# One ordered list for the attention and the start of the MLP, with the layer norm and the first weights in it

## The chip, the core and the metric

The kernel runs on one core of a Trainium2 chip. The metric is the device time of one launch in microseconds (us), lower is better. Times of single instructions are in nanoseconds (ns). The engines are named as in the profile: PE (TensorE, matmuls and transposes), DVE (VectorE), ACT (ScalarE), POOL (GpSimd) and SP (SyncE, which issues the loads and stores).

## The reference

Three stages in a row, with 4 batches, 8 heads, 576 tokens and a model width of 512:

```python
# 1. local attention: 4 heads see the last 32 tokens, 4 heads every 4th of the last 128
scores = np.where(masks[None], scale * np.matmul(q, k.transpose(0, 1, 3, 2)), -1e9)
attn = np.exp(scores - scores.max(-1, keepdims=True))
attn = attn / (np.sum(attn, axis=-1, keepdims=True) + 1e-09)
x = np.matmul(attn, v)                       # then heads side by side: (4, 576, 512)
# 2. mixture of 4 causal attention experts, 2 of 4 chosen for each token by a gate
a = softmax(causal(scale * (x @ wq[e]) @ (x @ wk[e]).T))
out += mask[..., None] * w[:, :, kk:kk + 1] * (a @ (x @ wv[e]) @ wo[e])
# 3. layer norm and MLP with a residual
xn = (x - mu) / np.sqrt(var + 1e-06) * g_ln
return x + np.maximum(xn @ w_ch1, 0.0) @ w_ch2
```

The two MLP weights arrive as 64-bit floats.

## The kernel before

Stage 1 runs in windows of three blocks of 64 queries by 96 keys for two heads (`window`, 48 of them). A window subtracts the row maximum on DVE, takes the exponential on ACT, sums on DVE (L439), adds 1e-9 to the sums on DVE (L441), takes the reciprocal (L443), multiplies on DVE or POOL (L445), transposes on PE and multiplies by the values. Stage 2 projects the result to values and gate (`value_tile`, tile `pv`), and to queries and keys (`project`, tile `pp`, L609); `attend` makes scores `s`, the softmax (L694 to L728), the transposes `ph` and `ppt` and the product `py`; `out_proj` (L823, tile `pwo`) gives the tokens `x2a` and `x2b` and their mean and variance. Values that need more than one pass are kept as a high and a low part, so most products are three matmuls.

Stage 3 works on 18 tiles of 128 tokens in five groups, `gi` 0 to 3 of four tiles and `gi` 4 of two. `norm` takes the mean off (tile `xg`, a single buffer, L971), transposes on PE (`pxt`, L974) and splits the result in high and low part (`xn`, ACT L982 and DVE L983). The hidden width is cut in 16 pieces `f`; each piece has two weight blocks which `decode` turns from 64-bit words into high and low parts: one step on ACT (L910), then DVE, POOL, DVE, ACT and POOL in turn (L911 to L922). `mlp_group` makes the hidden values (`phid`, L998), a ReLU in two parts (`ht`, L1005 and L1006), the output (`pout`, L1016) and adds it to the tokens on DVE (L1018). `inverse_std` has one POOL power (L946).

What sets the order: stages 1 and 2 are generators that ask for one operation at a time, with an engine (or a choice of two), a cost in ns and the times of what they depend on. `run_chains` always takes the operation that could begin first by these costs, at equal times the one with the lower rank, and the order in which it takes them is the order of each engine's instructions (`manual_schedule`). Stage 3 of the kernel before is recorded behind that list, as streams whose shares are set by the table `PRM`, and the layer below the kernel puts these instructions where its own scheduler wants them; they begin among the attention steps of the last batch. After its first three groups for `f` 0 to 2, the rest of stage 3 is a list of jobs in a fixed order, the same in both kernels: pieces 0 and 1 for groups 3 and 4, then piece 3, then pieces 2 and 3, then pairs of pieces for all five groups.

Of the kernel before, what the change touches and what calls it, by code (L numbers as in the profile page):

```python
# [23 lines left out]
def windowed_attention_moe_mlp(  # L24
# [20 lines left out]
    P = 128  # L45
# [110 lines left out]
    places = {"a": [0.0] * BANKS["a"], "s": [0.0] * BANKS["s"], "t": [0.0] * BANKS["t"]}  # L156
    facts, chains, mode = {}, [], [None]
# [38 lines left out]
    def run_chains():  # L196
        while chains:
# [50 lines left out]
    def attention_weights(x):  # L248
# [36 lines left out]
    places.update(nat=[0.0] * 2, vt=[0.0] * 2, qT=[0.0] * 2, sc=[0.0] * 5, pT=[0.0] * 2, xh=[0.0] * XB)  # L285
# [110 lines left out]

    def window(b, hp, u):
# [35 lines left out]
        sc = win.tile([P, TU, 96], F32, tag="sc", name="sc", bufs=5)  # L433
# [10 lines left out]
        t, e = yield either(("DVE", 370.0), ("POOL", 620.0), deps=[t])  # L444
# [8 lines left out]
        give("sc", t)  # L453
        pT = win.tile([96, TU * P], F32, tag="pT", name="pT", bufs=2)
# [37 lines left out]
    def value_tile(b, i):  # L492
# [19 lines left out]
        yield op("DVE", 75.0, [t, tv])  # L512
        nc.vector.tensor_copy(Gb[:m, i], pv[:m, E * D:NV])
# [3 lines left out]
        else:  # L517
# [63 lines left out]
    def project(b, pr_):  # L581
# [18 lines left out]
        for hf in range(2):  # L600
            for wh, wl, isq in ((wkh, wkl, False), (wqh, wql, True)):
# [10 lines left out]
                done_x(b, t)  # L612
                ends = []
# [37 lines left out]
    def attend(b, pr_, i):  # L651
# [64 lines left out]
        t = yield op("DVE", 75.0, tsum)  # L716
# [86 lines left out]
    def out_proj(b, i):  # L803
# [55 lines left out]
    phase_w.close()


    streams, done = {}, set()

    def add(key, gen, start, end, work):
        streams[key] = [gen, start, (end - start) / work]

    def step(key):
        st = streams[key]
        try:
            st[1] += next(st[0]) * st[2]  # L870
        except StopIteration:
            del streams[key]
            done.add(key)

    def need(key):
        while key not in done:
            step(key)

    def run_until(end):
        while streams:  # L880
            key = min(streams, key=lambda x: streams[x][1])
            if streams[key][1] >= end:
                break
            step(key)

    def after(keys, make):
        for key in keys:
            need(key)
        yield from make()


    wts = ctx.enter_context(tc.tile_pool(name="wts", bufs=1, side="right", reuse_waits="tile"))
    GF = 2
    groups = [range(a, min(a + 4, NTT)) for a in range(0, NTT, 4)]
    EARLY = 3
    g_in = wts.tile([P, KC], F32, name="g_in")
    nc.sync.dma_start(g_in, g_ln.rearrange("(c p) -> p c", p=P))
    w1v = w_ch1.bitcast(I32)
    w2v = w_ch2.bitcast(I32)

    def decode(src, hi, lo, gain):

        nl, nh = src[:, :, 0], src[:, :, 1]
        sq = wts.tile([P, DM], F32, tag="d_sq", name="d_sq", bufs=1)
        t1 = wts.tile([P, DM], I32, tag="d_t1", name="d_t1", bufs=1)
        pw = wts.tile([P, DM], I32, tag="d_pw", name="d_pw", bufs=1)
        nc.scalar.activation(sq, nh.bitcast(F32), AF.Square)  # L910
        nc.vector.tensor_scalar(t1, nh, 3, 0x3FFFFFF8, op0=ALU.logical_shift_left, op1=ALU.bitwise_and)  # L911
        nc.vector.scalar_tensor_tensor(t1, nh, -0x40000000, t1, op0=ALU.bitwise_and, op1=ALU.bitwise_or)  # L912
        nc.vector.tensor_scalar(pw, t1, -0x800000, None, op0=ALU.bitwise_and)
        pf = pw.bitcast(F32)
# [194 lines left out]
```

## Time and profile before

| | |
|---|---|
| median of 3 runs | 785.63 us (783.86 to 786.97) |
| the profiled execution | 782.97 us |
| its span, first to last instruction | 780.9 us |
| PE busy | 731.1 us (94%) |
| DVE busy | 555.5 us (71%) |
| ACT busy | 296.5 us (38%) |
| POOL busy | 212.4 us (27%) |
| mean granted TensorE clock | 0.980 |

The profiled execution took 2.07 us beyond its span. Busy time is the time in which at least one instruction of the engine ran; a busy PE can still run below its best rate. The granted clock is a share of 2.4 GHz.

### The profile page before, as it was taken

The numbers are of one execution on the slowest core, as the hardware profiler recorded it, in microseconds if no ns is written. First come the engines' busy times: TensorE is split into PE (matmuls) and PEld (weight loads), VectorE is DVE, ScalarE is ACT, GpSimd is POOL, SyncE is SP. The second block draws the span as 40 slices with busy tenths as digits, with TensorE's granted clock in tenths as the row PEclk, the third lists the DMA queues.
The fourth block names the chain that finished last, engine by engine and source line by source line (L and its number), as shares of the span: only waits on it lengthen the run. The fifth ranks groups of instructions, "written<-read, shape, count | busy, mean of one in ns | idle before, by whom it ended". The sixth has DMA issues, their size and how long they took to land.

```text
span 780.9 us, 13839 instructions
## 1 busy us (share of the span) xinstructions
PE 731.1 (94%) x5196; PEld 607.2 (78%) x5196; DVE 555.5 (71%) x1420; ACT 296.5 (38%) x796; POOL 212.4 (27%) x247
## 2 busy tenths in 40 slices
PE   6698989998998878799999999999999999999997
PEld 5577768987897667677778788888888888888886
DVE  5776988699968899889667897866466475553333
ACT  3455756556655654545224222222121121211110
POOL 3151422113412344333202344424033141220000
PEclk9979989999999989999999999999999999999999
DMA  7671323213120201101000121211011020000114
GB/s 150 130 145 39 74 64 68 52 41 82 42 54 13 65 28 55 55 1 55 1 1 28 54 81 56 81 54 60 22 54 55 4 78 27 28 1 0 40 69 134
DMA packets 87889, 41.79 MB, mean 54 GB/s; under 512 B 74384, under 2 KB 83088, under 8 KB 87824
## 3 DMA queue, kind: packets, MB, share of 16 engines
q1 hardware_dynamic: 87824, 40.92, 19.9%
q8 instruction: 41, 0.67, 0.4%
q14 instruction: 24, 0.20, 0.1%
HBM read 36.19 MB, written 4.72 MB: 52 GB/s over the span
## 4 chain that ended last, share of the span: by engine, by line
PE 70%; DVE 20%; ACT 4%; issue 2%; DMA 1%; POOL 1%; SPq 1%; DVEq 0%; POOLq 0%; ACTq 0%
PE phid L998 25%; PE pout L1016 25%; PE pp L609 4%; PE pwo L823 3%; PE ppt L750 2%; DVE sc L434 2%; DVE mx L431 2%; DVE sm L439 2%; DVE xl L484 1%; PE pv L508 1%; PE py L772 1%; DVE nm L694 1%; PE ppt L452 1%; DVE SQ L621 1%; PE ptr L372 1%
## 5 line engine op out<-in xcount | busy, mean ns | idle before, releaser
L1016 PE MATMUL pout<-wp,ht 128*128 128x512 f32 x864 | 215.8, 395 | 0.3 <-DVE ht L1006 0.3
L998 PE MATMUL phid<-xn,wp 128*128 128x512 f32 (+1 forms) x960 | 214.8, 372 | 0.0
L998 PEld LDWEIGHTS phid<-xn,wp 128*128 128x128 f32 x960 | 168.9, 188 | 34.8 <-DVE xn L983 0.2
L1016 PEld LDWEIGHTS pout<-wp,ht 128*128 128x128 f32 x864 | 160.2, 188 | 36.6 <-DVE ht L1006 0.8
L1018 DVE SCALAR_TENSOR_TENSOR x2a<-pout,rstd,x2a 128x512 f32<-128x512 f32 x124 | 88.4, 745 | 77.6 <-PE pout L1016 77.3
L1005 ACT ACTIVATE ht<-phid 128x512 fp32r<-128x512 f32 (+1 forms) x80 | 44.4, 555 | 222.3 <-PE pout L1016 137.0
L922 POOL TENSOR_TENSOR wp<-d_pw,wp 128x512 fp32r<-128x512 f32 x34 | 46.9, 1380 | 139.8 <-ACT wp L921 128.8
L728 POOL TENSOR_SCALAR Pp<-Pp,rs 128x128 f32<-128x128 f32 (+3 forms) x44 | 49.9, 1138 | 112.5 <-DVE rs L721 67.3
L1006 DVE SCALAR_TENSOR_TENSOR ht<-phid,ht 128x512 fp32r<-128x512 f32 (+1 forms) x80 | 50.1, 632 | 39.0 <-ACT ht L1005 38.8
L916 POOL TENSOR_TENSOR d_pw<-d_pw,d_t 128x512 f32<-128x512 f32 x34 | 44.0, 1294 | 70.1 <-DVE d_pw L915 57.8
L445 POOL TENSOR_TENSOR sc<-sc,rs 128x288 f32<-128x288 f32 x38 | 25.2, 670 | 85.0 <-DVE rs L443 36.7
L234 ACT COPY pT<-ppt 96x384 f32<-96x384 f32 (+4 forms) x79 | 35.9, 461 | 14.6 <-PE ppt L750 10.5
L696 ACT ACTIVATE Pp<-s,nm 128x192 f32<-128x192 f32 (+3 forms) x64 | 30.3, 474 | 23.4 <-DVE nm L694 19.7
L921 ACT CAST wp<-d_pw 128x512 fp32r<-128x512 f32 x34 | 21.1, 620 | 42.0 <-DVE d_pw L917 35.3
L679 PE MATMUL s<-KH,SQ 128*128 128x64 f32 (+4 forms) x96 | 34.0, 362 | 2.7 <-ACT Pp L696 2.3
L910 ACT ACTIVATE d_sq<-ws 128x512 f32<-128x512 f32 x34 | 22.9, 674 | 35.0 <-DVE d_pw L917 29.8
L452 PE MATMUL ppt<-ident,sc 128*96 128x128 f32 x144 | 25.5, 294 | 10.8 <-POOL sc L445 7.0
L372 PE MATMUL ptr<-ident,nat 72*128 72x72 f32 (+1 forms) x196 | 25.4, 253 | 10.5 <-DMA nat<-in_q_dram 8.3
L912 DVE SCALAR_TENSOR_TENSOR d_t<-ws,d_t 128x512 int32<-128x512 int32 x34 | 34.5, 1016 | 0.6
L423 PE MATMUL s<-kT,qT 64*64 64x96 f32 x576 | 34.1, 258 | 0.3 <-ACT kT L234 0.2
L750 PE MATMUL ppt<-ident,Pp 128*128 128x128 f32 x160 | 30.3, 290 | 3.0 <-DVE klz L630 1.3
L423 PEld LDWEIGHTS s<-kT,qT 64*64 64x64 f32 x576 | 31.3, 145 | 0.9 <-issue 0.5
(164 smaller groups left out, 1377.5 us busy)
## 6 DMA issues: line engine op xcount, KB each, us to landing
ws<-in_moe_w_ch_dram SPq DMA_DIRECT2D x34, 512.0 KB, 3.4
nat<-in_q_dram SPq DMA_DIRECT2D x14, 288.0 KB, 3.5
nat<-in_k_dram SPq DMA_DIRECT2D x14, 288.0 KB
vt<-in_v_dram SPq DMA_DIRECT2D x16, 192.0 KB, 4.2
out_dram<-x2a SPq DMA_DIRECT2D x12, 256.0 KB, 2.1
vt<-in_v_dram SPq DMA_DIRECT2D x32, 48.0 KB, 2.0
out_dram<-x2b SPq DMA_DIRECT2D x4, 256.0 KB, 2.5
vt<-in_v_dram SPq DMA_DIRECT2D x16, 40.0 KB, 1.9
```

Source lines behind the costliest of these rows:

```text
L234: (nc.scalar.copy if engine == "ACT" else nc.vector.tensor_copy)(dst, src)
L423: nc.tensor.matmul(ps[z, 96 * tt:96 * (tt + 1)], qT[z, 64 * t_:64 * t_ + 64], kT[z, 64 * t_:64 * t_ + 96], start=False, stop=tt == TU - 1)
L728: (nc.vector if e == "DVE" else nc.gpsimd).tensor_scalar(Ps[ee][:m, 64:n], Ps[ee][:m, 64:n], rs[:m, ee:ee + 1], None, op0=ALU.mult)
L750: nc.tensor.transpose(pt[:, P * (j - 1):P * j], Ps[ee][:, k0:k0 + P], ident)
L912: nc.vector.scalar_tensor_tensor(t1, nh, -0x40000000, t1, op0=ALU.bitwise_and, op1=ALU.bitwise_or)
L916: nc.gpsimd.tensor_tensor(pf, pf, t1.bitcast(F32), op=ALU.add)
L922: nc.gpsimd.tensor_tensor(lo, pf, hi.bitcast(F32), op=ALU.subtract)
L998: nc.tensor.matmul(ph[:, :n_tok], ws[:, c * P:(c + 1) * P], xs[c], start=n == 0, stop=n == 3 * KC - 1)
L1005: nc.scalar.activation(hh[:, :n_tok], ph[:, :n_tok], AF.Relu)
L1006: nc.vector.scalar_tensor_tensor(hl[:, :n_tok], ph[:, :n_tok], 0.0, hh[:, :n_tok].bitcast(F32), op0=ALU.max, op1=ALU.subtract)
L1016: nc.tensor.matmul(po, a_[:, sl], w_, start=n == 0, stop=n == 3 * len(fs) - 1)
L1018: nc.vector.scalar_tensor_tensor(x2(i), po, rstd[:, i:i + 1], x2(i), op0=ALU.mult, op1=ALU.add)
```

## The change

- **One list.** Opening the weights' memory, the decoding of the first three pieces (`decode`), `inverse_std`, `norm` for all five groups, and the first three groups for pieces 0, 1 and 2 become generators with costs, and go into the list of `run_chains` with ranks of 40 and more. The table `PRM` and the streams are gone. The jobs behind the list stay, run by a helper that takes the first engine of each choice.
- **Two engines' work in SBUF.** Operations of DVE and POOL that are marked with a star are not planned at the same time: each waits in the plan until the other's last starred one is over, plus 80 ns.
- **The window's sums.** A score tile gets a 97th column that holds 1e-9, written once in four lasting tiles (before: five buffers from a pool), and the sum runs over 97 columns; the separate addition (48 of them) is gone.
- **Engines.** Taking the mean off may go to ACT, with the sign turned and turned back behind the transpose; the copy of the gate's four columns may go to ACT.

```diff
+    shared = {"DVE": 0.0, "POOL": 0.0}
...
-                for engine, ns in engines:
+                for name, ns in engines:
+                    engine = name.rstrip("*")
                     at = max([free[engine]] + [d + lag[engine] for d in deps])
+                    if name != engine:
+                        at = max(at, shared["POOL" if engine == "DVE" else "DVE"])
...
+            if name != engine:
+                shared[engine] = at + ns + 80.0
...
+    SC = [win.tile([P, TU, 97], F32, name=f"sc{x}") for x in range(4)]
+    for sx in SC:
+        nc.gpsimd.memset(sx[:, :, 96:], 1e-9)
...
-        t = yield op("DVE", 363.0, [t])
-        nc.vector.tensor_reduce(sm, sc, axis=AX.X, op=ALU.add)
-        t = yield op("DVE", 75.0, [t])
-        nc.vector.tensor_scalar(sm, sm, 1e-9, None, op0=ALU.add)
+        t = yield op("DVE", 367.0, [t])
+        nc.vector.tensor_reduce(sm, sx, axis=AX.X, op=ALU.add)
...
-        yield op("DVE", 75.0, [t, tv])
-        nc.vector.tensor_copy(Gb[:m, i], pv[:m, E * D:NV])
+        _, e = yield either(("ACT", 178.0), ("DVE", 75.0), deps=[t, tv])
+        copy_by(e, Gb[:m, i], pv[:m, E * D:NV])
...
+    def norm_tile(gi, x):
+        i = groups[gi][x]
+        tn = yield key("xnp", gi)
+        t = yield key("st", i)
...
+        t, e = yield either(("ACT", 610.0), ("DVE*", 400.0), deps=[t, ta])
+        if e == "ACT":
+            nc.scalar.activation(xg, x2(i), AF.Identity, bias=mva[:, i, 0:1], scale=-1.0)
+        else:
+            nc.vector.tensor_scalar(xg, x2(i), mva[:, i, 0:1], -1.0, op0=ALU.subtract, op1=ALU.mult)
...
+        chain(40.0, open_mlp())
+        for f in range(3):
+            for x in range(2):
+                chain(41.0 + 2 * f + x, decode(f, x))
...
+        for gi in range(len(groups)):
+            chain(40.5 + gi, norm(gi))
+            for x in range(len(groups[gi])):
+                chain(41.2 + gi + 0.1 * x, norm_tile(gi, x))
+        for gi in range(EARLY):
+            chain(44.0 + gi, mlp_group((0, 1), gi, "a", "a"))
+            chain(48.0 + gi, mlp_group((2,), gi, "a", "a"))
         run_chains()
```

In `norm`, the groups 3 and 4 borrow memory of the attention, and the generator waits for every `py` of the last batch before it lets their tiles begin.

**How the order moves.** First place: PE where the first hidden values stand (`phid`, of token group 0). Before, the last projections of the last batch (`pp`) are over, and all 24 matmuls of a kind follow:

```order
L770 MATMUL py<-pTh,V_4206 64x128 x4
L772 MATMUL py<-pT_5249,V_4206 64x128
L772 MATMUL py<-pT_5264,V_4206 64x128
L679 MATMUL s_5291<-KH,SQ 128x448
L680 MATMUL s_5291<-klz_942,SQ 128x448
L682 LDWEIGHTS ident_bf
L682 MATMUL s_5291<-mdiag,ident_bf 128x128
L974 MATMUL pxt<-ident,xg 128x128 x4
L998 MATMUL phid<-xn_5777,wp 128x512
```

In the changed kernel they come in threes between the attention's transposes and scores, with projections of the last batch still to follow:

```order
L624 MATMUL pp<-xh_2902,wql 128x288
L751 MATMUL ph<-ident,Ph 128x128
L1043 MATMUL phid<-xn_4620,wp 128x512
L1043 MATMUL phid<-xn_4621,wp 128x512
L1043 MATMUL phid<-xn_4620,wp 128x512
L767 MATMUL ppt_5137<-ident,Pp 128x128 x4
L696 MATMUL s_5135<-KH,SQ 128x192
L697 MATMUL s_5135<-klz_924,SQ 128x192
L699 LDWEIGHTS ident_bf
L699 MATMUL s_5135<-mdiag,ident_bf 128x128
```

Eighteen `phid` matmuls now stand ahead of the last `pp`, where there were none.

Second place: PE at the end of the attention. Before, the last output projection (`pwo`) is followed by outputs of piece 2 (`pout`) with the transposes of group 3 (`pxt`) spread among them:

```order
L823 MATMUL pwo<-woh,yh_5242 128x512
L823 MATMUL pwo<-wol,yh_5242 128x512
L823 MATMUL pwo<-woh,yl_5243 128x512
L1016 MATMUL pout<-wp,ht 128x512 x3
L998 MATMUL phid<-xn_6180,wp 128x512 x2
L1016 MATMUL pout<-wp,ht 128x512 x3
L974 MATMUL pxt<-ident,xg 128x128 x4
L1016 MATMUL pout<-wp,ht 128x512 x3
```

Now the outputs of piece 2 are all done, and the transposes of groups 3 and 4 stand in a row:

```order
L1068 MATMUL pout<-wp,ht 128x512 x3
L840 MATMUL pwo<-woh,yh_5290 128x512
L840 MATMUL pwo<-wol,yh_5290 128x512
L840 MATMUL pwo<-woh,yl_5291 128x512
L840 MATMUL pwo<-woh,yh_5290 128x512
L840 MATMUL pwo<-wol,yh_5290 128x512
L840 MATMUL pwo<-woh,yl_5291 128x512
L1008 MATMUL pxt<-ident,xg 128x128 x16
L1043 MATMUL phid<-xn_6134,wp 128x512 x2
L1008 MATMUL pxt<-ident,xg 128x128 x4
L1043 MATMUL phid<-xn_6136,wp 128x512
```

Ahead of the last `pwo` there are 21 `pout` more than before and 16 `pxt` fewer.

Third place: DVE of the changed kernel just behind that, the second half of the stretch in which it makes the low parts of group 3 (`xn`), with the steps of the next weights (`d_pw`, `d_t`) between:

```order
L1019 SCALAR_TENSOR_TENSOR xn_6137<-pxt,xn_6135 128x2x128
L1003 TENSOR_SCALAR xg<-x2b_5833,mva 128x512
L935 SCALAR_TENSOR_TENSOR d_pw<-d_sq,d_pw 128x512
L920 TENSOR_SCALAR d_t_6258<-ws 128x512
L1019 SCALAR_TENSOR_TENSOR xn_6136<-pxt,xn_6134 128x2x128
L922 SCALAR_TENSOR_TENSOR d_t_6258<-ws,d_t_6258 128x512
L1019 SCALAR_TENSOR_TENSOR xn_6137<-pxt,xn_6135 128x2x128
L1003 TENSOR_SCALAR xg<-x2b_6104,mva 128x512
L1019 SCALAR_TENSOR_TENSOR xn_6136<-pxt,xn_6134 128x2x128
L926 TENSOR_SCALAR d_pw<-d_t_6258 128x512
L929 SCALAR_TENSOR_TENSOR d_pw<-ws,d_pw 128x512
L1019 SCALAR_TENSOR_TENSOR xn_6137<-pxt,xn_6135 128x2x128
```

From the first to the last of the eight `xn` steps of group 3 there are 18 DVE instructions; before, the additions of `pout` stood between them.

## Rows read from the trace of the kernel before

**Rows 1.** Windows by stage; busy us (x instructions) by engine, granted clock, DMA.
```profile
0.00:280.00 280.00, 247.69 (x2764) 212.27 (x2765) 222.68 (x780) 161.21 (x495) 80.59 (x146) 0.96 0.32 71
280.00:340.00 60.00, 48.92 (x350) 41.40 (x349) 54.46 (x146) 31.96 (x88) 24.76 (x20) 0.91 0.14 45
340.00:420.00 80.00, 78.42 (x452) 60.97 (x451) 58.53 (x144) 30.29 (x84) 17.14 (x13) 1.00 0.05 14
420.00:460.00 40.00, 39.66 (x186) 32.18 (x185) 34.26 (x58) 11.26 (x23) 17.33 (x13) 1.00 0.18 55
460.00:781.00 321.00, 316.41 (x1451) 260.41 (x1449) 185.56 (x294) 61.83 (x108) 72.57 (x57) 1.00 0.15 49
```

**Rows 2.** The chain that ended last by engine, whole span, and by line from 460 us.
```profile
PE 70%; DVE 20%; ACT 4%; issue 2%; DMA 1%; POOL 1%; SPq 1%; DVEq 0%; POOLq 0%; ACTq 0%
...
by line: PE pout L1016 50.5%; PE phid L998 48.0%; DVE x2b L1018 0.2%; DVEq L1105 0.2%; issue 0.0%
```

**Rows 3.** The chain in order of time: 24 hidden-value matmuls in the MLP.
```profile
488.94 5.53 PE phid L998 x24
```

**Rows 4.** The windows view in finer cuts around two places.
```profile
280.00:300.00 20.00, 16.34 (x105) 14.42 (x103) 18.72 (x46) 10.55 (x25) 9.23 (x8) 0.83 0.18 54
300.00:320.00 20.00, 14.95 (x108) 12.82 (x109) 18.77 (x51) 10.04 (x28) 8.60 (x7) 0.91 0.16 53
400.00:420.00 20.00, 20.00 (x123) 15.86 (x122) 13.79 (x33) 7.91 (x21) 1.57 (x1) 1.00 0.00 1
420.00:440.00 20.00, 20.00 (x103) 16.58 (x102) 17.46 (x31) 6.59 (x15) 9.52 (x7) 1.00 0.17 54
```

**Rows 5.** Views of single tiles: duration ns min/median/max, first and last start us.
```profile
L441 DVE TENSOR_SCALAR sm<-sm x48: 126/159/773, 12.8 to 268.8; 128x3 f32<-128x3 f32 x48
L717 DVE TENSOR_SCALAR sm<-sm x40: 138/169/812, 75.6 to 405.7; 128x2 f32<-128x2 f32 x40
L721 DVE TENSOR_TENSOR rs<-rs,gw x40: 123/160/995, 77.4 to 406.1; 128x2 f32<-128x2 f32 x40
L911 DVE TENSOR_SCALAR d_t<-ws x34: 414/420/427, 281.4 to 684.0; 128x512 int32<-128x512 int32 x34
L912 DVE SCALAR_TENSOR_TENSOR d_t<-ws,d_t x34: 678/694/1797, 281.9 to 684.5; 128x512 int32<-128x512 int32 x34
L922 POOL TENSOR_TENSOR wp<-d_pw,wp x34: 1265/1306/1785, 291.5 to 692.4; 128x512 fp32r<-128x512 f32 x34
L910 ACT ACTIVATE d_sq<-ws x34: 653/674/695, 280.9 to 684.2; 128x512 f32<-128x512 f32 x34
```

**Rows 6.** Groups by shape on DVE: busy us, mean ns, then idle before.
```profile
L441 DVE TENSOR_SCALAR sm<-sm 128x3 f32<-128x3 f32 x48 | 10.3, 216 | 0.3
L717 DVE TENSOR_SCALAR sm<-sm 128x2 f32<-128x2 f32 x40 | 8.7, 217 | 1.2 <-ACT Pp L696 0.7
L721 DVE TENSOR_TENSOR rs<-rs,gw 128x2 f32<-128x2 f32 x40 | 7.7, 194 | 0.5
L971 DVE TENSOR_SCALAR xg<-x2a,mva 128x512 f32<-128x512 f32 x14 | 8.7, 621 | 0.6 <-PE pxt L974 0.4
L971 DVE TENSOR_SCALAR xg<-x2b,mva 128x512 f32<-128x512 f32 x4 | 1.9, 482 | 2.8 <-PE pxt L974 2.8
L983 DVE TENSOR_TENSOR xn<-pxt,xn 128x256 fp32r<-128x256 f32 x20 | 8.0, 412 | 0.2 <-ACT xn L982 0.2
L917 DVE SCALAR_TENSOR_TENSOR d_pw<-d_sq,d_pw 128x512 f32<-128x512 f32 x34 | 23.3, 684 | 10.5 <-POOL d_pw L916 10.5
```

**Rows 7.** The same groups, DVE from 280 to 420 us only.
```profile
L912 DVE SCALAR_TENSOR_TENSOR d_t<-ws,d_t 128x512 int32<-128x512 int32 x8 | 6.7, 842 | 0.0
```

**Rows 8.** Timeline at 305 us: start, us, engine, line; a POOL and a DVE step.
```profile
305.31 1.16 POOL L920 TENSOR_TENSOR d_pw<-d_pw,g_in 128x512 f32<-128x512 f32 x1 [1.18 <-DVE d_pw L917]
...
305.75 1.27 DVE L912 SCALAR_TENSOR_TENSOR d_t<-ws,d_t 128x512 int32<-128x512 int32 x1
```

**Rows 9.** Timeline of PE around 417 us, transposes of one tile.
```profile
415.17 0.66 PE L974 MATMUL pxt<-ident,xg 128*128 128x128 f32 x4
```

More of the change, by code (lines that the diff above doesn't have):

```diff
@@ L526, in value_tile @@
             nc.vector.tensor_copy(V0[64:, :, D:], pe[:, :, D:])
-            t = yield op("DVE", 75.0, [t])
-            nc.vector.tensor_copy(Gb[64:, i], pv[:m, E * D:NV])
+            t, e = yield either(("ACT", 178.0), ("DVE", 75.0), deps=[t])
+            copy_by(e, Gb[64:, i], pv[:m, E * D:NV])
         give("t", t)
         put("vt", b, i, at=t)
+        if b == B - 1 and last("wv", NT):
+            give("ht", t, 2)
     def done_x(b, t):
@@ L612, in project @@
                 done_x(b, t)
+                if b == B - 1 and last("wqk", 8):
+                    put("wqk", at=t)
                 ends = []
@@ L834, in out_proj, with open_mlp @@
         nc.vector.bn_stats(st, x2(ti))
-        yield op("DVE", 90.0, [t])
+        t = yield op("DVE", 90.0, [t])
         nc.vector.bn_aggr(mva[:, ti], st)
+        put("st", ti, at=t)
+    GF = 2
+    groups = [range(a, min(a + 4, NTT)) for a in range(0, NTT, 4)]
+    EARLY = 3
+    w1v = w_ch1.bitcast(I32)
+    w2v = w_ch2.bitcast(I32)
+    WP = {}
+    HT = [(prj, "wvh"), (prj, "wvl")]
+    places.update(ht=[], ws=[], dsq=[], dt1=[], dpw=[], xg=[])
+    def open_mlp():
+        t = 0.0
+        for hp in range(NHP):
+            t = max(t, (yield key("x", B - 1, hp)))
+        phase_w.close()
+        wts = WP["wts"] = ctx.enter_context(tc.tile_pool(name="wts", bufs=1, side="right", reuse_waits="tile"))
+        WP["g_in"] = wts.tile([P, KC], F32, name="g_in")
+        yield op("SP", 500.0, [t])
+        nc.sync.dma_start(WP["g_in"], g_ln.rearrange("(c p) -> p c", p=P))
+        HT.append((wts, "h"))
+        for tag, n in (("ht", 1), ("ws", 2), ("dsq", 1), ("dt1", 1), ("dpw", 1), ("xg", 1)):
+            give(tag, t, n)
+        put("wts", at=t)
@@ L838, in windowed_attention_moe_mlp, with in_turn @@
+    def in_turn(*gens):
+        for g in gens:
+            yield from g
     with tc.manual_schedule():
@@ L857, in windowed_attention_moe_mlp @@
             chain(-9.0 + x, attention_weights(x))
-        run_chains()
[L859 to L914, printed above, removed]
-        nc.vector.scalar_tensor_tensor(pf, nl.bitcast(U32), 2.0 ** -52, pf, op0=ALU.mult, op1=ALU.mult)
-        nc.gpsimd.tensor_tensor(pf, pf, t1.bitcast(F32), op=ALU.add)
-        nc.vector.scalar_tensor_tensor(pf, sq, 2.0 ** -30, pf, op0=ALU.is_ge, op1=ALU.mult)
-        if gain:
-            pc = pf.rearrange("p (c n) -> p c n", c=KC)
-            nc.gpsimd.tensor_tensor(pc, pc, g_in[:, :, None].to_broadcast([P, KC, P]), op=ALU.mult)
-        nc.scalar.copy(hi, pf)
-        nc.gpsimd.tensor_tensor(lo, pf, hi.bitcast(F32), op=ALU.subtract)
@@ L1056, in windowed_attention_moe_mlp @@
[L1056 to L1063 removed]
+        chain(40.0, open_mlp())
+        for f in range(3):
+            for x in range(2):
+                chain(41.0 + 2 * f + x, decode(f, x))
+        chain(41.5, inverse_std(0, 4 * EARLY))
+        chain(41.5, inverse_std(4 * EARLY, NTT))
+        for gi in range(len(groups)):
+            chain(40.5 + gi, norm(gi))
+            for x in range(len(groups[gi])):
+                chain(41.2 + gi + 0.1 * x, norm_tile(gi, x))
@@ L1069, in windowed_attention_moe_mlp, with weights @@
         jobs += [((f0, f0 + 1), gi) for gi in range(len(groups))]
+    def weights(fs):
+        for f in fs:
+            for x in range(2):
+                run(decode(f, x))
+                yield
     fill = weights((3,))
     for x, (fs, gi) in enumerate(jobs):
-        if fs[-1] not in WF:
-            run(fill)
+        if (fs[-1], 0) not in WF:
+            for _ in fill:
+                pass
         if x == 0 or fs != jobs[x - 1][0]:
             if fs != (2, 3):
-                run(fill)
+                for _ in fill:
+                    pass
                 nf = fs[-1] + 1 if fs[-1] > 1 else 3
```

334 lines of the change are left out of this document (197 added, 137 removed).

## The prediction

> **What bounds the kernel now.** I read the windows by stage first, then the chain of waits, then single tiles. In the windows the reader is to see two kernels behind one another. From 460 us on PE is busy 316 of 321 us at full clock [rows 1], and the chain of waits there is PE alone, 50.5% and 48.0% for the two matmuls of the MLP [rows 2]; 24 of them take 5.53 us, so 0.23 us each [rows 3]. Nothing in the change touches these matmuls or the jobs that order them, so this stage stays as it is. Ahead of it lie 460 us in which PE and DVE take turns. PE has 32 us of idle time up to 280 us and 11.1 us (60.0 less 48.9) from 280 to 340 us, where DVE is busy 54.5 of 60 us; from 340 to 420 us PE is busy 78.4 of 80 [rows 1]. So whatever the change can win it wins ahead of 340 us, and it must bring the last attention step forward or put MLP matmuls into that idle time.
>
> How much a microsecond less of DVE is worth there I take from the chain: DVE holds 20% of it, 156 us, practically all ahead of 460 us [rows 2]. DVE's busy time up to 460 us is 222.7 + 54.5 + 58.5 + 34.3 = 370 us [rows 1]. So 42% of DVE's work lies on the path that sets the end. In the same way ACT has 4%, 31 us, of 234.7 us busy: 13%. I price DVE work at 0.42 and ACT work at 0.13 of its length. The bounds are 0 (PE takes over wherever DVE gives way) and 1 (DVE is the only bound).
>
> **What leaves DVE.**
> - The addition of 1e-9, 48 times, 10.3 us in all [rows 6]. The sum over three columns more adds some 3 ns for each of 48, nothing. The four fills of the new column stand on POOL among its fills of the first microseconds, long ahead of the first sum.
> - Waits of DVE behind POOL. The timeline shows one: POOL's step runs from 305.31 to 306.47 us, and DVE's L912, begun at 305.75, takes 1.27 us [rows 8] where its median is 0.694 [rows 5]. The reader finds such waits by means far above medians: L717, 217 against 169 ns, 40 times, 1.9 us; L721, 194 against 160, 1.4 us; L912, 842 against 694 for the 8 up to 420 us, 1.2 us [rows 5 to 7]. Together 4.5 us; those of L441 are in its 10.3 already. The plan keeps such pairs apart by costs, and real times drift from costs, so I take half, 2.3 us, between 0 and 4.5.
> - Taking off the mean: the order has 13 of 18 on ACT. A mean of (8.7 + 1.9) / 18 = 0.59 us [rows 6] makes 7.7 us.
> - Nine copies of gate columns go to ACT too: by the nearest small DVE step, 0.169 us [rows 5], 1.5 us. Other choices between engines move by a few each way, and I take them at nothing.
>
> Together 21.8 us less DVE, at 0.42 a gain of 9.2 us, between 0 and 21.8. ACT gets 13 steps that I price by L910, which also reads 512 columns of SBUF, 0.674 us [rows 5], and nine small ones at about 0.2: 10.6 us, at 0.13 a loss of 1.4 us.
>
> On these waits the Trainium skill has a rule: by its page SBUF — State Buffer, section Who interferes with whom, DVE and POOL share a pair of ports under an exclusive lock, and the one that starts first holds it for its whole instruction. This case's trace agrees: L912 above ended only after POOL had. By the rule alone the list could remove all 4.5 us and not half, 0.9 us more; but it adds that issue order decides who blocks, and the order on two engines is fixed here only within each.
>
> **What moves on PE.** Eighteen hidden-value matmuls now stand ahead of the last projections of the last batch, where PE had 11.1 us of idle time [rows 1]: 18 times 0.23 is 4.2 us that no longer lies behind 340 us. I take it whole, between 0 (they wait there themselves) and 4.2. What is queued behind them is the attention's transposes and scores; if a weight is late, these wait. The 21 outputs that moved ahead of the last `pwo` moved from one busy stretch to another, and are worth nothing.
>
> The granted clock in this stretch is 0.83 from 280 to 300 us and 0.91 from 300 to 320 [rows 4], so PE ran at the lower of its two levels (1.2 GHz) for 6.8 and 3.6 us, after it had been idle on and off; that cost half of it, 5.2 us of work. With more matmuls there part of this may go: I take 2 us, between 0 and 5.2.
>
> **What is late next.** Before, PE loses nothing at the attention's end, 20.00 of 20 us busy on both sides of the last `pwo` near 419 us [rows 4], because outputs of piece 2 fill in while group 3 is being normed. In the new order nothing is left to fill: behind the last `pwo` come 20 transposes and then `phid` matmuls, which need the low parts of all four tiles of group 3. These are eight of 18 DVE steps in a row: 8 at 0.41, seven of the decoding (three at 0.42 as L911, four at 0.69 as L912 and L917), two `xg` at 0.48 and one small one. That is 3.3 + 1.3 + 2.8 + 1.0 + 0.2 = 8.6 us [rows 5, 6], and the statistics of the last tile stand in front of them. The first matmuls can go some 1.5 us before the last of these steps. PE has about 5 times 0.6 us of transposes to do meanwhile [rows 9] and the statistics delay the whole; I put the hole at 6 us, between 2 (DVE's steps begin before the last `pwo` ends) and 11 (POOL's steps between them wait, and the clock falls).
>
> **Sum.** -9.2 (DVE) + 1.4 (ACT) - 4.2 (matmuls moved) - 2 (clock) + 6 (hole) = -8.0 us. Against the profiled execution's own 782.97 us that is 775.0 us; this execution lies 2.7 us below the median of the runs, 785.63 us, so for a median I say 777.6 us.
>
> **The rivals.**
> - DVE is the only bound ahead of 340 us (for it: it is busy 54.5 of 60 us from 280 to 340; against it: up to 280 us it is idle for 57 of 280 us [rows 1]). Then its relief counts whole, 21.8 in place of 9.2 us, and the moved matmuls fall into the idle time that this uses up: -21.8 + 1.4 - 2 + 6 = -16.4, 769 us; with the hole at its lower bound 765 us.
> - No change. PE takes over where DVE gives way: PE is on the chain with 70% [rows 2]. The relief counts a quarter, 5.5 us, the moved matmuls and the clock give nothing, the hole costs 6: 787 us at most, and 784 with a hole of 3.
> - Slower, by one mechanism: `phid` waits for its weights in the middle of the attention. PE works in order, and the first piece took from 280.9 us (its step on ACT) to 291.5 + 1.3 = 292.8 us (its last on POOL) [rows 5], 12 us over four engines. The list places `phid` by costs; wherever PE comes earlier than the weights, projections and scores of the last batch stand behind it. From 8 us of such waits in all the gain is gone; 12 us, one full passage, gives 785.6 - 8 + 12 = 790 us. For it speaks that ranks decide only between equal times, so nothing holds MLP steps back from the attention's path; against it that the memory for these weights opens at the same step as before, when the last windows end.
> - The hole is longer. PE's clock fell after pauses of the kind it would be [rows 4]; one fall costs up to 3.4 us more, 781 us. The Trainium skill says the same on its page TensorE: Matmul & The Clock Gate, section HAM oscillation — how this bites in real kernels: a wait in the middle of a stream of matmuls lets the gate fall back to half rate, and the next matmuls start cold. No row shows what a single pause of 6 us does here.
>
> **How the numbers follow.** The forecast has 0.48, the first rival 0.20, no change 0.16, the late weights 0.10, the longer hole 0.06. A measurement of this kernel cannot tell less than about 0.5%, 3.9 us, from no change. Of the forecast's own range, 770 to 784 us, about a tenth lies inside that bound; so faster has 0.43 + 0.20 + 0.02 = 0.65, the same 0.05 + 0.13 + 0.04 + 0.01 = 0.23, slower 0.12. The range goes from the first rival's lower price to the slower one's: 764 to 789 us.
>
> **What would show it.** In the profile of the changed kernel: L441 gone, and the means of the softmax's small DVE steps nearer to their medians (about 170 ns). The last `pwo` near 419 - 14 = 405 us on the same scale. PE busier than 49 of 60 us in the stretch that ends with the last projections, with `phid` in it. Behind the last `pwo` a stretch of some 8 us in which PE does little but `pxt`, with DVE on `xn` and `d_pw`. From there on PE busy throughout, and the same time from the first `phid` of group 3 to the end. The prediction is wrong if PE's idle time ahead of the last `pwo` is as large as before, if waits of `phid` or `pout` for `wp` appear among the attention's steps, or if the hole is filled by work that I took to be used up.

## The result and the profile after

| | before | after |
|---|---|---|
| median of 4 runs (us) | 785.04 (783.86 to 786.97) | 777.09 (775.04 to 778.78) |
| ratio, 95% interval | | 0.9902 [0.9882, 0.9922] |
| the profiled execution, its span (us) | 782.97, 780.9 | 777.57, 775.8 |

The changed kernel is 1.0% faster. The two profiled executions differ by less than the medians, by 5.4 us, because that of before lies 2.1 us below its median and that of after 0.5 above; what is read from the traces below can account only for the 5.1 us between their spans. The page of the changed kernel's profile begins with the span and the busy times; the third line is the chain that ended last, by engine:

```profile
span 775.8 us, 13793 instructions
...
PE 728.6 (94%) x5196; PEld 606.8 (78%) x5196; DVE 535.2 (69%) x1357; ACT 303.4 (39%) x817; POOL 207.0 (27%) x245
...
PE 71%; DVE 20%; ACT 5%; DMA 2%; issue 2%; POOL 1%; DVEq 0%; SPq 0%; ACTq 0%; POOLq 0%
```

DVE lost 20.3 us of busy time (it had 555.5) and ACT gained 6.9, and yet DVE still has 20% of the chain, as in [rows 2]. The windows by stage of after, with the columns of [rows 1], and below them finer cuts around the attention's end:

```profile
0.00:280.00 280.00, 249.88 (x2780) 215.48 (x2781) 214.70 (x744) 161.22 (x503) 77.23 (x146) 0.96 0.35 71
280.00:340.00 60.00, 56.18 (x401) 47.28 (x400) 52.97 (x145) 38.08 (x106) 26.32 (x21) 0.94 0.11 36
340.00:420.00 80.00, 71.75 (x412) 55.55 (x411) 57.88 (x136) 33.83 (x85) 19.40 (x16) 0.96 0.09 27
420.00:460.00 40.00, 39.71 (x189) 32.71 (x188) 32.11 (x55) 12.32 (x23) 17.64 (x14) 0.99 0.21 66
460.00:776.00 316.00, 311.07 (x1422) 255.77 (x1420) 177.57 (x281) 57.99 (x103) 66.46 (x52) 1.00 0.14 47
...
412.00:416.00 4.00, 1.52 (x8) 1.13 (x8) 3.00 (x7) 1.87 (x5) 2.35 (x2) 0.78 0.33 114
416.00:420.00 4.00, 2.76 (x10) 1.91 (x9) 3.71 (x9) 2.22 (x6) 1.69 (x2) 0.50 0.07 22
420.00:424.00 4.00, 4.00 (x17) 3.21 (x16) 4.00 (x7) 1.38 (x4) 2.42 (x2) 0.86 0.43 131
```

From 280 to 340 us PE is busy 56.2 of 60 us where it was busy 48.9 [rows 1]; from 340 to 420 us it is busy less, 71.75 against 78.42, and the finer cuts show part of why: a hole at 412 to 420. The last stage is PE alone, as before. The timeline of PE shows the hole (start, us, engine, line; in brackets the idle time before and what ended it):

```profile
408.73 0.39 PE L840 MATMUL pwo<-woh,yl 128*128 128x512 f32 x1
408.96 0.60 PE L1008 MATMUL pxt<-ident,xg 128*128 128x128 f32 x4
411.21 0.65 PE L1008 MATMUL pxt<-ident,xg 128*128 128x128 f32 x4 [1.65 <-ACT xg L1001]
413.82 0.74 PE L1008 MATMUL pxt<-ident,xg 128*128 128x128 f32 x4 [1.96 <-ACT xg L1001]
415.21 1.11 PE L1008 MATMUL pxt<-ident,xg 128*128 128x128 f32 x4 [0.65 <-DVE xg L1003]
417.57 1.22 PE L1043 MATMUL phid<-xn,wp 128*128 128x512 f32 x2 [1.24 <-ACT xn L1017]
```

The last `pwo` stands at 409, not 419 us. Then PE does only the transposes of group 3, each behind its `xg`, and waits 1.65 + 1.96 + 0.65 + 1.24 = 5.5 us before and at the first `phid`. What PE waits for in the whole span (us in total, times, longest):

```profile
PE ptr L380 <- DMA nat<-in_q_dram: 9.6, 3, 4.8
PE pxt L1008 <- ACT xg L1001: 3.6, 2, 2.0
PE ppt L464 <- DVE xl L497: 3.5, 7, 1.3
...
PE ph L751 <- DVE Ph L740: 2.0, 3, 0.8
...
PE ppt L464 <- POOL sc L457: 1.7, 5, 0.6
...
PE s L696 <- ACT Pp L713: 1.1, 3, 0.5
```

No line of this view names `wp`, the weights. So of the span's 5.1 us, 10.4 were won up to the last `pwo` (its end went from 419.5 to 409.1 us) and 5.3 lost behind it. In PE's time: up to the last `pwo` it idles 2.2 us less ahead of 280 us and 6.1 us less from there on, and is busy 2.1 us less; behind it, it idles 5.7 us more and is busy 0.4 us less.

### The profile page after: what moved, and what is told of

Its sections match the earlier page's. It is cut to its first block, busy times and chain, and to the rows that moved or that the text cites. A ratio compares the mean times of both kernels' runs of the same rounds, so it can differ in the third digit from the quotient of the medians.

```text
span 775.8 us, 13793 instructions
## 1 busy us (share of the span) xinstructions
PE 728.6 (94%) x5196; PEld 606.8 (78%) x5196; DVE 535.2 (69%) x1357; ACT 303.4 (39%) x817; POOL 207.0 (27%) x245
## 4 chain that ended last, share of the span: by engine, by line
PE 71%; DVE 20%; ACT 5%; DMA 2%; issue 2%; POOL 1%; DVEq 0%; SPq 0%; ACTq 0%; POOLq 0%
PE pout L1068 26%; PE phid L1043 25%; PE pp L624 3%; PE pv L521 2%; PE pwo L840 2%; PE ppt L767 2%; PE s L436 2%; DVE nm L711 1%; PE ptr L380 1%; PE ppt L464 1%; DMA nat<-in_k_dram 1%; DVE xl L497 1%; DVE klz L647 1%; DVE sc L448 1%; DVE mx L446 1%
## 5 line engine op out<-in xcount | busy, mean ns | idle before, releaser
L1043 PE MATMUL phid<-xn,wp 128*128 128x512 f32 (+1 forms) x960 | 218.0, 374 | 2.3 <-ACT xn L1017 1.2
L745 POOL TENSOR_SCALAR Pp<-Pp,rs 128x512 f32<-128x512 f32 (+3 forms) x38 | 45.6, 1207 | 71.0 <-DVE rs L738 37.6
L380 PEld LDWEIGHTS ptr<-ident,nat 72*128 72x128 f32 (+1 forms) x196 | 20.6, 155 | 15.4 <-DMA nat<-in_q_dram 5.2
L922 DVE SCALAR_TENSOR_TENSOR d_t<-ws,d_t 128x512 int32<-128x512 int32 x34 | 32.1, 944 | 0.6
```

Source lines behind the costliest of these rows:

```text
L380: nc.tensor.transpose(pt[:, pw * c:pw * (c + 1)], nat[:, hf * ch + c].rearrange("p h d -> p (h d)"), ident[:pw, :pw])
L745: (nc.vector if e == "DVE" else nc.gpsimd).tensor_scalar(Ps[ee][:m, 64:n], Ps[ee][:m, 64:n], rs[:m, ee:ee + 1], None, op0=ALU.mult)
L1043: nc.tensor.matmul(ph[:, :n_tok], ws[:, c * P:(c + 1) * P], xs[c], start=n == 0, stop=n == 3 * KC - 1)
```

## The experiments

All kernels here keep the whole computation. The table puts them side by side: the ratio to the kernel before, run on the same chip; from each profile the end of the last `po` (end of the windows' products) and of the last `pwo`, PE's idle time from 280 us to there, and what is left of the span behind it, all in us. Two ratios to before are compared by dividing them; such a quotient is good to about 0.25% (2 us). The other columns come from one execution each, which lies between 2.1 us below the median of its kernel's times (before) and 3.5 us above it (e6). They scatter too: after, e4, e5 and e8 have the same order on every engine up to the last `po`, and yet it ends between 269.1 and 272.9 us.

| kernel | ratio [95%] | last `po` | last `pwo` | PE idle | behind |
|---|---|---|---|---|---|
| before | 1 | 277.1 | 419.5 | 12.7 | 361.4 |
| after | 0.9902 [0.9882, 0.9922] | 272.5 | 409.1 | 6.6 | 366.7 |
| e2, addition back | 0.9948 [0.9934, 0.9962] | 275.5 | 412.0 | 5.4 | 366.1 |
| e3, no star | 1.0046 [1.0028, 1.0064] | 281.3 | 414.1 | 13.4 | 373.0 |
| e6, one cost 145 | 1.0010 [0.9994, 1.0026] | 276.6 | 420.4 | 9.8 | 365.8 |
| e1, list alone | 1.0062 [1.0050, 1.0074] | 278.6 | 419.5 | 12.2 | 366.1 |
| e4, hole filled | 0.9834 [0.9815, 0.9853] | 271.4 | 401.1 | 4.7 | 368.7 |
| e8, two `xg` | 0.9953 [0.9935, 0.9971] | 272.9 | 413.0 | 9.0 | 365.2 |
| e5, `xg` on DVE | 0.9904 [0.9887, 0.9921] | 269.1 | 405.5 | 5.8 | 367.9 |
| e7, before with column | 1.0115 [1.0096, 1.0134] | 281.0 | 430.4 | 15.3 | 364.7 |
| f1, addition, same order | 0.9996 [0.9982, 1.0010] | 277.9 | 414.8 | 6.7 | 366.2 |
| f2, column, same order | 0.9999 [0.9986, 1.0013] | 280.3 | 422.9 | 13.4 | 361.6 |
| n1, before, cost 145 | 1.0075 [1.0057, 1.0092] | 282.2 | 430.2 | 14.6 | 360.5 |
| n2, one cost 138 | 1.0071 [1.0054, 1.0088] | 279.6 | 420.5 | 9.4 | 365.9 |

### Parts of the change undone, and one cost nudged

**The addition back in the list**, told to the planner:

```diff
-        t = yield op("DVE", 367.0, [t])
-        nc.vector.tensor_reduce(sm, sx, axis=AX.X, op=ALU.add)
+        t = yield op("DVE", 363.0, [t])
+        nc.vector.tensor_reduce(sm, sc, axis=AX.X, op=ALU.add)
+        t = yield op("DVE", 75.0, [t])
+        nc.vector.tensor_scalar(sm, sm, 1e-9, None, op0=ALU.add)
```

> The changed kernel with the separate addition of 1e-9 put back in the windows (48 steps on DVE, some 10 us), all else as changed. Theory (42% of DVE's work is on the path): 4 us slower than the changed kernel, 781 us. Rival 1 (DVE is the only bound there, its work counts whole): 10 us slower, 787 us. Rival 2 (PE takes over, DVE's relief is worth nothing): 777 us.

Measured: 779.67 us, 3.6 us slower than after (0.9948 / 0.9902). That is near 0.42 of the addition's 10.3 us, but the list also came out in another order.

**No exclusion of DVE and POOL in the plan:**

```diff
-                    if name != engine:
-                        at = max(at, shared["POOL" if engine == "DVE" else "DVE"])
...
-            if name != engine:
-                shared[engine] = at + ns + 80.0
```

> The changed kernel without the rule that plans the SBUF work of DVE and POOL apart, all else as changed. Theory (half of 4.5 us of waits avoided, at 0.42): 1 us slower than the changed kernel, 778 us, with the means of the small softmax steps on DVE back near 200 ns from about 185. Rival (the whole of the waits, at their full length): 4 to 5 us slower, 782 us.

Measured: 788.07 us, 11 us slower than after. The small softmax steps on DVE got longer, as expected: their means are 231 and 220 ns here, 205 and 175 in after. That is 2.8 us for 40 of each, and no account of 11.

**One cost nudged.** `MODE` is the time that the plan adds when PE changes between kinds of tile; no engine's work depends on it.

```diff
-    MODE = 141.0
+    MODE = 145.0
```

> The changed kernel with one planning cost nudged, which has no meaning of its own: the cost of a change of PE's mode is 145 in place of 141, so that the list takes some steps in another order. Theory (the gain comes from what work there is): within 2 us of the changed kernel, 775 to 779 us. Rival (a list of this kind lands by chance, and the gain is one such chance): more than 4 us away.

Measured: 784.42 us, 8.5 us slower than after, by four nanoseconds in a plan. The expectation that the order would move the time by at most 2 us fell. The windows view of this kernel's profiled execution, the slowest of its twelve (787.94 us), shows a loss ahead of the attention's end, in both stretches:

```profile
0.00:280.00 280.00, 245.56 (x2725) 209.72 (x2726) 212.29 (x729) 158.01 (x493) 69.49 (x136) 0.96 0.36 71
280.00:340.00 60.00, 51.26 (x364) 43.41 (x363) 49.00 (x130) 34.79 (x90) 17.61 (x15) 0.94 0.11 36
```

PE did 4.3 us less work up to 280 us than in after, and 4.9 us less in the next 60; DVE and ACT were no busier. More waiting, not more work.

**The list alone:** the addition back, no star, `xg` and the gate copies on DVE.

```diff
-                    if name != engine:
-                        at = max(at, shared["POOL" if engine == "DVE" else "DVE"])
...
-        t, e = yield either(("ACT", 610.0), ("DVE*", 400.0), deps=[t, ta])
+        t, e = (yield op("DVE*", 400.0, [t, ta])), "DVE"
```

> The changed kernel with only the one list left: the addition back, no rule that keeps DVE and POOL apart, the mean taken off on DVE alone, the gate's copies on DVE. Theory: the matmuls moved ahead (-4), the clock (-2) and the hole behind the last output projection (+6) cancel, 785 us, as the kernel before, with the hole of 5 to 6 us in the trace. Rival (the list is what gains, the small parts give nothing): 777 to 779 us.

Measured: 788.36 us, slower than before. So moving the first groups into the list is no gain by itself in this order. The size of e6's loss forbids to read e1 and e3 as the price of the star.

### The hole, and single parts

**The hole filled.** The outputs of piece 2 for groups 1 and 2 are taken out of the list and recorded behind it, so that they stand behind the last `pwo`:

```diff
-            chain(48.0 + gi, mlp_group((2,), gi, "a", "a"))
+            if gi < 1:
+                chain(48.0 + gi, mlp_group((2,), gi, "a", "a"))
         run_chains()
...
+    for gi in range(1, EARLY):
+        run(mlp_group((2,), gi, "s", "t"))
```

> The changed kernel with the outputs of piece 2 for groups 1 and 2 taken out of the list and recorded behind it, ahead of the other jobs. In the order 24 of these output matmuls (5.5 us) now stand behind the last output projection, between the transposes of group 3. Theory (PE idles 5 to 6 us there for want of work): 4 to 5 us faster than the changed kernel, 772 to 773 us. Rival (DVE, with its 18 steps and now these outputs' additions as well, sets the end of this stretch): no faster, 777 us or more.

Measured: 771.2 us, the fastest kernel here; 0.9834 / 0.9902 = 0.9931, 5.4 us less than after. PE's timeline shows the outputs between the transposes:

```profile
400.74 0.39 PE L840 MATMUL pwo<-woh,yl 128*128 128x512 f32 x1
400.96 0.87 PE L1068 MATMUL pout<-wp,ht 128*128 128x512 f32 x3
401.67 0.60 PE L1008 MATMUL pxt<-ident,xg 128*128 128x128 f32 x4
402.03 2.32 PE L1068 MATMUL pout<-wp,ht 128*128 128x512 f32 x9
404.19 0.60 PE L1008 MATMUL pxt<-ident,xg 128*128 128x128 f32 x4
404.54 2.71 PE L1068 MATMUL pout<-wp,ht 128*128 128x512 f32 x9
407.65 0.66 PE L1008 MATMUL pxt<-ident,xg 128*128 128x128 f32 x4 [0.40 <-ACT xg L1001]
409.93 1.12 PE L1008 MATMUL pxt<-ident,xg 128*128 128x128 f32 x4 [1.62 <-DVE xg L1003]
411.52 1.22 PE L1043 MATMUL phid<-xn,wp 128*128 128x512 f32 x2 [0.47 <-ACT xn L1017]
```

The waits left are 0.40 + 1.62 + 0.47 = 2.5 us where after had 5.5. Up to 346 us the order on every engine is that of after, so here it was nearly held. Of the 6.0 us between the two spans, 3.0 us are the hole, 1.9 us are idle time of PE between 280 us and the last `pwo`, and 1.1 us are no more than the earlier last `po`: it ended that much earlier with the same instructions in the same order, so that this part is scatter between executions. Of the other 4.9 us the hole itself is six tenths; the rest came ahead of the last `pwo`, with two dozen outputs less there.

The clock fell here too, though PE waited less than half as long:

```profile
408.00:412.00 4.00, 1.91 (x8) 1.27 (x7) 4.00 (x10) 1.69 (x5) 1.24 (x1) 0.71 0.38 131
412.00:416.00 4.00, 4.00 (x13) 3.12 (x13) 2.90 (x7) 1.55 (x4) 2.01 (x2) 0.50 0.02 4
416.00:420.00 4.00, 4.00 (x18) 3.21 (x17) 3.28 (x5) 1.89 (x4) 1.98 (x2) 0.94 0.46 133
```

**Two buffers for `xg`** (`bufs=2`, the same in the count of free places):

```diff
-        xg = wts.tile([P, DM], F32, tag="xg", name="xg", bufs=1)
+        xg = wts.tile([P, DM], F32, tag="xg", name="xg", bufs=2)
```

> The changed kernel with two buffers for the tile from which the mean has been taken (xg), so that the next tile's step need not wait for the transposes of the one before. Theory (the hole is set by DVE's 18 steps in a row): PE's waits for xg (3.6 us) become waits for xn, at most 1 us faster, 776 to 777 us. Rival (the single buffer makes the hole): 3 to 4 us faster, 773 us.

Measured: 780.33 us, 4 us slower than after. In this kernel's timeline the transposes behind the last `pwo` go in pairs:

```profile
412.86 1.03 PE L1008 MATMUL pxt<-ident,xg 128*128 128x128 f32 x8
416.96 1.27 PE L1008 MATMUL pxt<-ident,xg 128*128 128x128 f32 x8 [3.07 <-ACT xg L1001]
419.24 1.22 PE L1043 MATMUL phid<-xn,wp 128*128 128x512 f32 x2 [1.01 <-ACT xn L1017]
```

The waits are 3.07 + 1.01 = 4.1 us where after had 5.5, so in this order the second buffer takes 1.4 us off the hole and leaves the rest. The loss lies in the new order ahead of it (last `pwo` 3.9 us later than in after, 2.4 us more of PE idle).

**`xg` on DVE alone**, all 18 of them:

```diff
-        t, e = yield either(("ACT", 610.0), ("DVE*", 400.0), deps=[t, ta])
+        t, e = (yield op("DVE*", 410.0, [t, ta])), "DVE"
```

> The changed kernel with the mean taken off on DVE for all 18 tiles (planned at 410 ns for 400), all else as changed. Theory (13 steps of 0.59 us back on DVE at 0.42, less what ACT is spared): 2 us slower than the changed kernel, 779 us. Rival (these steps lie in stretches where PE has the path): 777 us.

Measured: 777.11 us, the same as after, with DVE busy 541.9 us in place of 535.2. A loss of the 2 us that were expected would be at the edge of what the comparison can tell.

**The column in the kernel before**, planned anew: four lasting tiles with a 97th column, additions gone.

```diff
+    SC = [win.tile([P, TU, 97], F32, name=f"sc{x}") for x in range(4)]
+    for sx in SC:
+        nc.gpsimd.memset(sx[:, :, 96:], 1e-9)
...
-        nc.vector.tensor_reduce(sm, sc, axis=AX.X, op=ALU.add)
-        t = yield op("DVE", 75.0, [t])
-        nc.vector.tensor_scalar(sm, sm, 1e-9, None, op0=ALU.add)
+        nc.vector.tensor_reduce(sm, sx, axis=AX.X, op=ALU.add)
```

> The kernel before with the 97th column alone: 48 additions fewer on DVE, four lasting score tiles for five buffers, all else as before. Theory (42% of 10 us): 4 us faster than the kernel before, 781 us. Rival 1 (DVE's work counts whole): 775 us. Rival 2 (without the list the relief is lost in the order): 785 us.

Measured: 794.24 us, 9 us slower than before with 48 steps less. Again a new order, and one tile less than the five buffers of before. What a step costs can't be seen while its removal changes the list.

### The order held, and the order alone

**The addition in the changed kernel's own order:** issued, but not told to the planner, so that the attention's list stays word for word.

```diff
         t = yield op("DVE", 367.0, [t])
-        nc.vector.tensor_reduce(sm, sx, axis=AX.X, op=ALU.add)
+        nc.vector.tensor_reduce(sm, sc, axis=AX.X, op=ALU.add)
+        nc.vector.tensor_scalar(sm, sm, 1e-9, None, op0=ALU.add)
```

> The changed kernel with the addition of 1e-9 issued again in every window, but not told to the planner: the order of the attention's instructions stays that of the changed kernel, and DVE has 48 steps more. Theory (42% of DVE's work is on the path): 4 us slower than the changed kernel, 781 us. Rival (DVE's work counts whole): 10 us slower, 787 us. If the steps cost little at a fixed order (777 to 778 us), the earlier differences between lists came from their orders alone.

Measured: 784.69 us, 0.9996 / 0.9902 = 1.0095, 7.4 us slower than after. The added steps in this kernel's groups (busy us, mean ns), the windows' first stage, and two of PE's waits:

```profile
L454 DVE TENSOR_SCALAR sm<-sm 128x3 f32<-128x3 f32 x48 | 11.7, 245 | 1.6
```

```profile
0.00:280.00 280.00, 242.46 (x2743) 208.11 (x2744) 219.36 (x775) 157.65 (x492) 75.86 (x143) 0.97 0.36 71
```

```profile
PE ppt L465 <- POOL sc L458: 4.6, 8, 0.8
...
PE ph L752 <- DVE Ph L741: 3.2, 5, 1.1
```

DVE has 11.7 us more to do there, and PE, which was busy 249.9 us up to 280, is busy 242.5; its waits for `sc` and `Ph`, both steps behind DVE's softmax, grew from 1.7 and 2.0 us to 4.6 and 3.2. In this order 0.6 of the added work (7.4 of 11.7 us) reached the end.

**The column in the kernel before's own order:** five lasting tiles, no addition, the planner told as before.

```diff
+    SC = [win.tile([P, TU, 97], F32, name=f"sc{x}") for x in range(5)]
...
         t = yield op("DVE", 75.0, [t])
-        nc.vector.tensor_scalar(sm, sm, 1e-9, None, op0=ALU.add)
```

> The kernel before with the 97th column and without the 48 additions, five lasting score tiles, and the planner told as before, so that the attention's order stays that of the kernel before. Theory: 4 us faster than the kernel before, 780 to 781 us. Rival (whole): 775 us. If the nine microseconds that the column cost in the kernel before came from the work itself and not from the new order, it is slower here too, above 790 us.

Measured: 784.61 us, ratio 0.9999 [0.9986, 1.0013]: nothing. The same window of this kernel:

```profile
0.00:280.00 280.00, 249.81 (x2743) 214.63 (x2745) 214.80 (x722) 159.81 (x489) 78.40 (x149) 0.94 0.35 67
```

DVE is 7.9 us less busy than before up to 280 us [rows 1], and the last `po` is 3.2 us later, not earlier. PE is busy 2.1 us longer for its work there, at a granted clock of 0.94 in place of 0.96. But the clock alone did not eat the gain: among the runs with a mean granted clock of 0.978 to 0.980, four of this kernel take 783.1 us on the mean and seven of before 783.8, 0.7 us where 4 were expected.

The profiles say the same of f1 and f2 once one source of scatter is left out. Near 40 us each of these kernels waits for a load, and that wait ends at another time in each execution. The transposes behind it, in before, f2, after and f1:

```profile
38.59 0.44 PE L372 MATMUL ptr<-ident,nat 96*128 96x96 f32 x3 [3.52 <-DMA nat<-in_q_dram]
40.76 0.71 PE L372 MATMUL ptr<-ident,nat 96*128 96x96 f32 x3 [2.87 <-DMA nat<-in_q_dram]
40.40 0.74 PE L380 MATMUL ptr<-ident,nat 96*128 96x96 f32 x3 [3.73 <-DMA nat<-in_q_dram]
40.15 0.74 PE L380 MATMUL ptr<-ident,nat 96*128 96x96 f32 x3 [4.12 <-DMA nat<-in_q_dram]
```

From their start to the end of the last `po` it takes 238.5 us in before and 239.6 in f2, 232.1 in after and 237.8 in f1. The other kernels with the order of after, e4, e5 and e8, take 232.1, 230.8 and 230.9 us. So adding the steps costs 5.7 us up to there (37 of the 48 lie behind the load, 8.5 us), and leaving them out in the order of before gains nothing.

**The nudge in the kernel before, and the other way in the changed one** (`MODE` 145 and 138):

```diff
-    MODE = 141.0
+    MODE = 145.0
```

> The kernel before with the same nudge of a planning cost (145 in place of 141). If lists land by chance with several us either way, this one is also some us away from the kernel before, to either side: 779 to 791 us. If the kernel before is robust and only the changed kernel's order was lucky, within 2 us: 783 to 787 us.

```diff
-    MODE = 141.0
+    MODE = 138.0
```

> The changed kernel nudged the other way (138 in place of 141). By chance alone 775 to 787 us; if the first nudge hit a bad order and the changed kernel's own is the usual one, 775 to 779 us.

Measured: 789.77 us, 5.9 us slower than before; 789.88 us, 13 us slower than after. The changed kernel at 138 waits in the middle of the attention's steps; its PE waits:

```profile
PE ppt L464 <- POOL sc L457: 6.0, 8, 1.3
PE s L696 <- ACT Pp L713: 4.9, 7, 2.2
```

After had 1.7 and 1.1 us of these. From 280 to 340 us PE is busy 46.5 us in the nudged kernel before and 54.1 us in the nudged changed one, where it was 48.9 [rows 1] and 56.2 without the nudge:

```profile
280.00:340.00 60.00, 46.52 (x308) 40.28 (x308) 53.24 (x141) 28.33 (x80) 26.20 (x20) 0.86 0.14 45
```

```profile
280.00:340.00 60.00, 54.06 (x405) 46.88 (x404) 52.72 (x152) 37.02 (x103) 25.21 (x23) 0.97 0.12 41
```

So one design gave 777.1, 784.4 and 789.9 us by a number that means nothing to the engines, and the design of before 785.0 and 789.8. The table shows where: in nine of the ten kernels with the list the time behind the last `pwo` is 365.2 to 368.7 us, while the last `pwo` itself wanders from 401.1 to 420.5. (The tenth is e3, whose order puts fewer outputs of the MLP ahead of it.)

## Why the prediction was right, and where it was not

The number was right: 8.0 us less were predicted, 7.95 measured between the medians. Not all of its reasons were, and the profiled execution, forecast at 775.0 us, took 777.57. The ends of the range, 764 and 789 us, stand 1 us below the 765 and 790 us that the prediction's own rivals give.

- **What bounds the kernel: shown.** Behind 460 us nothing changed (PE busy 311 of 316 us). What tells one list from another lies ahead of the last `pwo`, as the table shows.
- **The matmuls moved ahead of the last `pp`: seen in the profile.** PE is busy 56.2 us from 280 to 340 us, `phid` begins at 313.9 and not at 339.6 us, and PE's idle time from 280 us to the last `pwo` fell from 12.7 to 6.6 us, 6.1 us, where 4.2 were predicted. It stayed lower, at 4.7 to 9.8 us, in all lists with the star; in the two without it (e1, e3) it is 12.2 and 13.4 us. The last `pwo` came 10.4 us earlier, not 14.
- **The hole: shown, in place and size.** 6 us were predicted, 5.5 to 5.8 measured (5.8 with the small gaps behind it), and e4, which fills more than half of it, is 5.4 us faster, 3.0 us of it there. The clock fell with it, as the rival of a longer hole had it, but less: the granted clock is 0.78, 0.50 and 0.86 in the three cuts from 412 to 424 us, which puts PE at the lower of its two levels for 1.8, 4.0 and 1.1 us of them. It was busy then for at least 2.8 + 1.1 and at most 1.5 + 2.8 + 1.1 us, and half of such time is lost: 1.9 to 2.7 us, where the rival had up to 3.4. On this the Trainium skill's page TensorE: Matmul & The Clock Gate, section HAM oscillation — how this bites in real kernels, says that a wait in the middle of a stream of matmuls lets the gate fall to half rate and that the next ones start cold; this trace agrees, with 0.50 at 416 us after the pauses from 409 us on.
- **DVE's relief at 0.42: the step that failed.** The work left DVE as predicted, 20.3 us of 21.8, and ACT got 6.9 us of 10.6. But there is no fixed share of it on the path. With the order held, the additions cost 7.4 us in the order of after, 0.6 of their length, and their removal gave 0 in the order of before, 0.7 us among runs at the same clock, where 0.42 would have given 4; `xg` back on DVE cost nothing that shows (e5, in a new order), and what ACT's part cost no run tells. The -9.2 us is no sum of such parts; 0.42 lies between the ends measured, that is all. The chain's share of an engine is no price: it says how often the engine was last, not how close the next one was behind.
- **DVE's waits behind POOL: fewer in the small steps, not in the decoding.** The groups of after show the softmax's small steps at 205 and 175 ns (mean, behind the busy us), where [rows 6] has 217 and 194, and taking off the mean on ACT at 726 ns where I had priced 674:

```profile
L734 DVE TENSOR_SCALAR sm<-sm 128x2 f32<-128x2 f32 x40 | 8.0, 205 | 0.9 <-ACT Pp L713 0.6
L738 DVE TENSOR_TENSOR rs<-rs,gw 128x2 f32<-128x2 f32 x40 | 6.9, 175 | 0.6
...
L1001 ACT ACTIVATE xg<-x2a,mva 128x512 f32<-128x512 f32 x12 | 8.7, 726 | 0.0
```

  That is 40 × (12 + 19) ns = 1.2 us for the two, of 3.3 that the prediction saw in them. The star bears on them: without it they have means of 231 and 220 ns (e3) and 223 and 219 (e1), in the eight lists with it 173 to 218 and 156 to 209. The decoding's step took 740 ns for 9 of them from 280 to 420 us, 842 in [rows 7], which would make 2.1 us in all where 2.3 were predicted; but this one is no work of the star, since its mean is 685 ns without it in e3 and 957 ns with it in e5. Whether any of these waits reached the end, no experiment here tells.
- **The clock ahead of the attention's end: not confirmed.** It rose from 0.91 to 0.94 from 280 to 340 us, which is worth 1.8 us at most, and fell from 1.00 to 0.96 from 340 to 420, the hole included.
- **The rivals.** DVE as the only bound fell with f2. Late weights did not happen: no wait for `wp` stands in the view. "No change" and "slower" are the times that the same design takes under other costs (784.4, 789.9 us), though by another way than I had written: by waits for the attention's own steps, not for the MLP's weights (n2 has one of those, 0.9 us).

What the change is worth is therefore settled only as a run: this list with this order is 1.0% faster. That another list of the same design would be faster than another of the design before is not shown. The lists with the star and the column run at 777.1, 784.4 and 789.9 us, or 771.2, 777.1 and 780.3 with one choice changed (e4, e5, e8); the kernels with streams at 784.6, 785.0, 789.8 and 794.2 us. The first are faster on the mean, but the ranges overlap, and e1 and e3 (788.4, 788.1 us, without the star) fit either reading; a handful of orders each would have to be run to price the star. And since e6 and n2 move the time by 8.5 and 13 us, I can't exclude that the 7.95 us owe more to the order than to the parts; the agreement of the sum with the time is partly chance.

## What to carry to other kernels

Where a planner's list sets the order of several engines, shift one meaningless cost by a few nanoseconds and run the result before crediting an edit: here that alone was worth 6 to 13 us, as much as the change. Price an edit with the order held, both by adding it to the new kernel and by removing it from the old one, since the two gave 7.4 and 0 us. Compare the times in two profiles from a common wait whose end scatters, not from the start of the span. And when a stage is moved forward, look at what used to fill the pause behind it: keeping back two dozen matmuls for that place gave 5.4 us, of which the trace shows 3.0 in the pause itself.

## What the runs showed of the hardware

- A pause of PE that was broken by transposes (idle 1.65, 1.96 and 0.65 us between blocks of 0.6 to 1.1 us) was enough for the granted clock to stand at 0.50 from 416 to 420 us; in the next 4 us, in which PE was busy throughout, it was 0.86, and over 420 to 460 us 0.99. With waits of only 0.40, 1.62 and 0.47 us in the same place (e4) it still stood at 0.71, 0.50 and 0.94 in three cuts of 4 us: filling half of the pause with matmuls did not keep the clock up.
- Forty-eight DVE steps of 128 by 3 elements had means of 216 ns in before [rows 6], 245 in f1 and 249 in e2 (the line below), with a shortest of 126 ns in before [rows 5]. Whether the plan knew of them made no difference to that: it did in e2 and did not in f1. What beside them lengthens them is not shown.
- The wait for one load near 40 us ended between 38.3 and 42.0 us in four kernels with the same order up to there (e5, e4, after, e8), and the last product of the windows moved with it.

```profile
L455 DVE TENSOR_SCALAR sm<-sm 128x3 f32<-128x3 f32 x48 | 11.8, 249 | 0.2
```
